# Fused attention and two MoE-style layers on one core: six chunks instead of seven in the first phase, two Strassen units of 768 tokens instead of one of 1024

## The chip, the core and the metric

The kernel runs on one core of a Trainium2 chip. Its time is the device time of that core in microseconds, and runs are compared by their median. TensorE (PE) does the matmuls; its weight loads are shown apart as PEld. VectorE (DVE), ScalarE (ACT) and GpSimd (POOL) do the elementwise work. SyncE (SP) issues nearly all DMAs, from one queue.

## The reference

All inputs are fp32. Attention without softmax has 8 batches, 8 heads, 576 positions and 64 features: `kv = k^T v` per head, `o = q kv`, then an RMS norm over the 64 features times `g_norm`. Its output, as 4608 tokens of 512 features, is `x`. Then:

```
a = x @ w1          # 512 x 1024
b = x @ w2          # 512 x 1024
x2 = ((a * b) @ w3) @ w_out          # 1024 x 1024, 1024 x 512
h = x2 @ moe2_w_in                   # 512 x 2048
out = (h * sigmoid(h)) @ moe2_w_out  # 2048 x 512
```

## The kernel before

Every fp32 matmul is made of three passes in the fp32r type, high x high, high x low and low x high, so each operand is split into a high and a low half (a cast on ScalarE, a subtraction on VectorE). The product `w3 @ w_out` is formed once at the start, so that the first layer is two matmuls: `a` and `b`, and `(a * b) @ wc`.

The 4608 tokens are 9 chunks of 512. **The first phase** computes the attention of all nine chunks. For the chunks in `PLAIN` it computes x2 at once by plain three-pass matmuls, in 8 steps a chunk. A step `j` has 12 matmuls into `pa`, 12 into `pb` and 12 into `x2ps` for the step before it (`g2_mm`), all 128x128 by 512 columns. ScalarE copies `pa` to `asb`, VectorE multiplies it with `pb`, and the product is split into `ch` and `cl`. The chunks in `LATER` only have their attention's output `x` stored to memory (`xd`).

Beside this the first phase converts weights for the second. A list of pieces (128x512 each) is worked off by `advance()`: load piece n+3, cast the high half of piece n-1 and scale piece n+1 on ScalarE, then on VectorE rebuild the bits of piece n (`cv_bits`), form Strassen sums where the piece is the second of its group (`block_sums`, role 1 of the roles 0, 1, 2), and subtract for the low half of piece n-1 (`cv_low`). The results are written to memory (`wbd`) by DMAs. The first 40 pieces belong to the resident weights. The 84 behind them are 28 groups of three: of kind "block" (two loads, the third piece has none) and, alternating with these for the first 24 groups, of kind "sum" (made from resident halves, no load). Between two steps' matmuls `ensure(done - 1)` calls `advance()` once: in each step behind `pa` ("piece A") and again behind the split of `ch` and `cl` ("piece B").

Attention is laid into this stream by hand. A gap is a third of a step; `event(gap, f, ...)` files a call under twice the gap, six such places a step, and `att_step(step, part)` calls what is filed. Part 0 comes behind `pa` (and takes what is filed for the last sixth of the step before too), part 1 behind piece A, part 2 behind the multiply of `pb` and `asb`, part 3 behind the split, part 4 behind `g2_mm`. Chunk c has these calls, in gaps from its base: `att_a`/`att_b` (q times kv, squares), `att_c` (sums of squares by matmul), `att_d` (ScalarE, the root), `att_e` (two VectorE operations and a split into `rh` and `rl`), `att_r` (spreads the root to PSUM banks `rb`), `att_x` (VectorE multiplies it on) and `att_f` (splits x, or stores it where c is in `LATER`). `kv_mm` makes the next batch's kv. All of these share two PSUM banks of the tag "att", which come round in the order of allocation.

**The second phase** takes x2, and for `LATER` first x, in units by one level of Strassen: seven products in place of eight. A unit has w columns for each half of its tokens, 2w tokens. Kind "A" runs the first layer for `LATER` (blocks a 0, b 0, a 1, b 1, out 0, out 1) and kind "B" the second layer (in 0 to 3, out 0 to 3). A block is 7 runs of 12 matmuls, 84 of w columns, and streams 7 weight tiles `w` of 512 KB. The last "out" block of a unit runs behind the first block of the next unit. On the engines every instruction is in the order in which the program issues it.

Of the kernel before, what the change touches and what calls it, by code (L numbers as in the profile page):

```python
# [16 lines left out]
B, H, S, D = 8, 8, 576, 64  # L17
# [6 lines left out]
NCH = NT // N  # L24
# [2 lines left out]
K2 = F2 // P  # L27
EPS = 1e-6

PLAIN = (0, 1, 2, 3, 5, 6, 7)  # L30
LATER = tuple(c for c in range(NCH) if c not in PLAIN)
UNITS = (("A", 512), ("B", 512), ("B", 512), ("B", 512), ("B", 384), ("B", 384))
HMAX = max(w for _, w in UNITS)
HOP = 512

# [38 lines left out]
def fused(ctx, tc, q, k, v, g, w1, w2, w3t, wo1, wb, out):  # L74
# [10 lines left out]
    def close(*names):  # L85
        for name in names:
            opened.pop(name).__exit__(None, None, None)
# [16 lines left out]
    def bank(tag, bufs, name):  # L104
        return ps.tile([P, N], F32, tag=tag, bufs=bufs, name=name)

    def split(h, l, x):
        nc.scalar.copy(out=h, in_=x)  # L108
        nc.vector.tensor_sub(out=l, in0=x, in1=h.bitcast(F32))
# [42 lines left out]
    done = 0  # L152
# [135 lines left out]
    def flush():  # L288
        due, writes[:] = list(writes), []
        for x in due:  # L290
            nc.sync.dma_start(**x)

    def advance():
        nonlocal done
        n = done
        flush()
        cv_load(n + 3)
        cv_high(n - 1)
        cv_scale(n + 1)
        cv_bits(n)  # L300
        block_sums(n)
        cv_low(n - 1)
        done += 1

    def ensure(n):

        while done < min(n + 2, len(pieces) + 1):
            advance()
# [134 lines left out]
    with tc.tile_pool(name="pro", bufs=2, side="right") as pro:  # L443
# [17 lines left out]
        for i in range(2 * K1):  # L461
            hf, j = divmod(i, K1)
# [24 lines left out]
        def w_out(m):  # L487
            split(wch[m], wcl[m], banks.pop(m))
# [66 lines left out]
    def g2_mm(c, j):  # L555
# [6 lines left out]
        if j == K1 - 1:  # L562
            for m in range(KD):
                if c != PLAIN[-1]:
                    o = at.tile([P, N], F32, tag="x2o", bufs=4, name=f"x2o{c}_{m}")
# [6 lines left out]
                else:  # L572
                    nc.scalar.copy(out=o, in_=x2ps[c][m])
                (nc.sync if c != PLAIN[-1] else nc.scalar).dma_start(out=x2d[c][:, m, :], in_=o)
            del x2ps[c]

    def g1_mm(ps_out, wh, wl, xh, xl):
        for kk in range(KD):
            s = slice(kk * P, (kk + 1) * P)
            passes(ps_out, wh[:, s], wl[:, s], xh[:, kk, :], xl[:, kk, :], kk == 0, kk == KD - 1)  # L580


    events = {}

    def event(gap, f, *args):
        events.setdefault(int(2 * gap), []).append(lambda: f(*args))

    gap = -6
    for c in range(1, NCH):
        if 1 < c < B:  # L590
            event(gap, kv_mm, c, [0, 1])
            event(gap, kv_load, c, [2, 3])
            event(gap + 3, kv_mm, c, [2, 3])
            event(gap + 3, kv_load, c, [4])
            event(gap + 6, kv_mm, c, [4])
            event(gap + 6, kv_out, c)
        if c + 1 < B:
            event(max(gap + 6, 2), kv_load, c + 1, [0, 1])
        if c > 1:
            for p in range(KD):  # L600
                event(gap_was + 11, q_load, c, p)
        for i in range(2):
            event(gap + 7 + 3 * i, att_a, c, i)
            event(gap + 7 + 3 * i, att_b, c, i)
        event(gap + 12, att_c, c)
        event(gap + 13, att_d, c)
        event(gap + 14, att_e, c)
        for i in range(2):
            event(gap + 17 + i, att_r, c, i)
            event(gap + 17 + i, att_x, c, i)  # L610
            event(gap + 17.5 + i + 1.5 * (c in LATER), att_f, c, i)
        gap_was = gap
        gap += 20 if c + 1 < B else 13

    def att_step(step, part):
        for n in range(6 * step + part - (part == 0), 6 * step + part + 1):
            for f in events.pop(n, ()):
                f()


    def b_pool(name, **more):
        return ctx.enter_context(tc.tile_pool(name=name, **{**dict(bufs=1, reuse_waits="tile"), **more}))


    blocks = []
    for u, (kind, _) in enumerate(UNITS):
        todo = ([("a", 0), ("b", 0), ("a", 1), ("b", 1), ("out", 0)] if kind == "A" else
                [("in", 0), ("in", 1), ("out", 0), ("in", 2), ("out", 1), ("in", 3), ("out", 2)])
        blocks.append((u, *todo[0]))
        if u > 0:  # L630
            blocks.append((u - 1, "out", NDB[UNITS[u - 1][0]] - 1))
        blocks += [(u, *x) for x in todo[1:]]
    blocks.append((len(UNITS) - 1, "out", NDB[UNITS[-1][0]] - 1))
    stream = [(b, n) for b in range(len(blocks)) for n in range(7)]
    wt = {}

    def w_load(at):
        if at >= len(stream):
            return
        b, n = stream[at]  # L640
        u, which, i = blocks[b]
        from_ = w_rest if at % WBUFS else w_first
        t = from_.tile([P, 2, 2, 2 * P], F32, tag="w", name=f"w{b}_{n}")
        nc.sync.dma_start(out=t, in_=wbd[i + WBD[(UNITS[u][0], which) if which == "out" else which]][:, RUNS[n][1]])
        wt[b, n] = t
# [4 lines left out]
    def half_pieces(u, h):  # L650

        kind, w = UNITS[u]
        t0 = 2 * sum(ww for k, ww in UNITS[:u] if k == kind) + h * w
# [8 lines left out]
    def x2_load(u):  # L662

        t = xr.tile([P, KD, 2, HMAX], F32, tag="x2r", name=f"x2r{u}")
        x2r[u] = t
        from_ = xd if UNITS[u][0] == "A" else x2d
        for h in range(2):
            for col, c, at0, n in half_pieces(u, h)[1]:
                for k0 in range(0, KD, 2):
                    r = slice(k0, k0 + 2)  # L670
                    yield nc.sync.dma_start(out=t[:, r, h, col:col + n], in_=from_[c][:, r, at0:at0 + n])
# [33 lines left out]
    def x2_ops(u):  # L705
        t, w = x2r.pop(u), UNITS[u][1]
        return Operands({f"b{i + 1}{h + 1}": t[:, 2 * i:2 * i + 2, h, :w] for i in range(2) for h in range(2)}, w,
                        lambda n: (x_first if n < 3 else x_rest).tile(
                            [P, 2, 2, HOP], F32R, tag=f"xo{n}", name=f"xo{u}_{n}"), f"x{u}",
                        [nc.gpsimd if u and n in (1, 3) else nc.vector for n in range(7)])  # L710

    prev = None
    for s_, c in enumerate(PLAIN):
        lastc = c == PLAIN[-1]
        xh, xl = xt.pop(c)
        for j in range(K1):
            step = s_ * K1 + j
            pa = bank("ab", 2, f"pa{c}_{j}")
            g1_mm(pa, w1h[j], w1l[j], xh, xl)
            att_step(step, 0)  # L720
            if s_ == 0 and j + 1 < K1:
                ensure(w12_piece[j + 1] - 1)
            elif not (lastc and j > 2):
                ensure(done - 1)
            att_step(step, 1)
            if s_ == 0 and j == 0:
                for m in range(half, K1):
                    w_out(m)
            asb = cp.tile([P, N], F32, tag="asb", bufs=1, name=f"asb{c}_{j}")
            nc.scalar.copy(out=asb, in_=pa)  # L730
            pb = bank("ab", 2, f"pb{c}_{j}")
            g1_mm(pb, w2h[j], w2l[j], xh, xl)
            ch = cp.tile([P, N], F32R, tag="ch", name=f"ch{c}_{j}")
            cl = cp.tile([P, N], F32R, tag="cl", name=f"cl{c}_{j}")
            nc.vector.tensor_mul(out=asb, in0=pb, in1=asb)  # L735
            att_step(step, 2)
            split(ch, cl, asb)
            ct[c, j] = ch, cl
            att_step(step, 3)
            if s_ == 0 and j + 1 < K1:  # L740
                ensure(w12_piece[j + 1])
            elif not (lastc and j > 2):
                ensure(done - 1)
            if lastc and j == 2:
                ensure(len(pieces))
            if lastc and j == 3:
                flush()
                nc.scalar.preload_act_table_set("silu_and_others")
                close("at", "cv", "stg")
                xr, w_first, tt, x_first = (b_pool(n) for n in ("xr", "w_first", "tt", "x_first"))  # L750
                list(x2_load(0))
                w_load(0)
            if lastc and j == 5:
                xops = {0: x2_ops(0)}
                xops[0].step(0)
                xops[0].sums()
            if lastc and j in (6, 7):
                xops[0].step(j - 5)
            if prev is not None:
                g2_mm(*prev)  # L760
            att_step(step, 4)
            prev = c, j
# [242 lines left out]
```

## Time and profile before

| | us |
|---|---|
| median of 3 runs | 1436.19 (1434.88 to 1437.12) |
| profiled execution | 1431.62 |
| its span, first to last instruction | 1429.5 |
| first phase, to the first matmul of the units | 609.7 |
| TensorE busy in the span | 1396.9 |
| VectorE busy | 916.2 |
| ScalarE busy | 665.1 |
| GpSimd busy | 311.6 |

The page gives for each engine the time in which an instruction of it ran. A matmul's row ends later than the next one starts, because they are pipelined, so its duration (390 ns) is not its cost; the distance from start to start is. The profiled execution is one run of its own, 4.6 us below the median of the others.

### The profile page before, as it was taken

The page shows a single profiled execution, that of the slowest core. Times are in us where ns is not written, and L with a number is a line of the kernel's source. Part 1 is how long each engine was busy: PE and PEld are TensorE (multiplying, and loading weights), DVE is VectorE, ACT ScalarE, POOL GpSimd, SP SyncE. Part 2 cuts the span into 40 slices and gives each one's busy share as a digit, 9 for nine tenths or more (in the row PEclk, how much of TensorE's full clock was granted, in tenths as well). Part 3 has the DMA queues.
Part 4 walks back from the last instruction along what each step waited for, and adds up shares of the span by engine and source line. Part 5 has one row for each costly group of instructions (what it writes and reads, how often), then busy time and mean ns, then how long its engine had stood idle before and what let it go on. Part 6 is the DMA issues. An engine that isn't in the chain of part 4 may idle for free.

```text
span 1429.5 us, 19284 instructions
## 1 busy us (share of the span) xinstructions
PE 1396.9 (98%) x7112; PEld 1150.0 (80%) x7112; DVE 916.2 (64%) x1263; ACT 665.1 (47%) x1064; POOL 311.6 (22%) x143
## 2 busy tenths in 40 slices
PE   7789999999999999999999999999999999999998
PEld 4567777777777777888878787887878789999998
DVE  7767475565656674343775668566865676678568
ACT  7766445443444562232535354443535354543443
POOL 0000000000000001104533526224532442345222
PEclk9999999999999999999999999999999999999999
DMA  9655566768595767076677666866686668878876
GB/s 334 226 174 171 193 205 229 255 211 278 195 296 179 254 197 269 18 244 199 193 232 266 191 191 203 295 193 185 193 287 194 189 205 288 288 244 253 287 246 205
DMA packets 149725, 320.05 MB, mean 224 GB/s; under 512 B 14208, under 2 KB 72576, under 8 KB 149632
## 3 DMA queue, kind: packets, MB, share of 16 engines
q1 hardware_dynamic: 149056, 317.78, 68.5%
q8 instruction: 57, 0.93, 0.3%
q10 hardware_dynamic: 576, 1.05, 0.2%
q14 instruction: 36, 0.29, 0.1%
HBM read 246.42 MB, written 72.35 MB: 223 GB/s over the span
## 4 chain that ended last, share of the span: by engine, by line
PE 93%; DVE 2%; DMA 2%; issue 1%; ACT 1%; SPq 0%; DVEq 0%; ACTq 0%
PE ps L795 56%; PE pb L113 4%; PE x2ps L113 4%; PE pa L113 4%; PE pb L115 4%; PE pb L114 3%; PE x2ps L115 3%; PE pa L115 3%; PE x2ps L114 3%; PE pa L114 3%; DMA raw<-w3t_l 1%; PE kvps L338 1%; PE o L370 1%; PE rb L419 1%; DVE z L201 1%
## 5 line engine op out<-in xcount | busy, mean ns | idle before, releaser
L795 PE MATMUL ps<-xo,w 128*128 128x512 f32 (+1 forms) x2016 | 425.4, 371 | 0.1
L795 PEld LDWEIGHTS ps<-xo,w 128*128 128x128 f32 x2016 | 368.8, 188 | 53.7 <-ACT u L827 1.3
L795 PE MATMUL ps<-go,w 128*128 128x512 f32 (+1 forms) x1848 | 392.4, 370 | 5.1 <-issue 5.1
L795 PEld LDWEIGHTS ps<-go,w 128*128 128x128 f32 x1848 | 335.8, 188 | 58.3 <-issue 12.2
L699 DVE TENSOR_TENSOR go<-g,go 128x1024 fp32r<-128x1024 f32 (+1 forms) x110 | 156.2, 1424 | 112.9 <-ACT go L698 112.5
L805 DVE TENSOR_TENSOR c<-ps,c 128x512 f32<-128x512 f32 (+1 forms) x260 | 154.3, 632 | 24.6 <-PE ps L795 24.4
L686 POOL TENSOR_TENSOR x_t<-x2r 128x1024 f32<-128x1024 f32 (+1 forms) x12 | 30.3, 2522 | 564.4 <-DMA w<-wbd 563.9
L686 POOL TENSOR_TENSOR g_t<-g 128x1024 f32<-128x1024 f32 (+1 forms) x44 | 113.0, 2569 | 108.6 <-ACT g L838 62.5
L698 ACT CAST go<-g 128x1024 fp32r<-128x1024 f32 (+1 forms) x110 | 105.0, 974 | 46.2 <-PE ps L795 35.0
L686 POOL TENSOR_TENSOR g<-g,g_t 128x1024 f32<-128x1024 f32 (+1 forms) x22 | 48.4, 2200 | 342.8 <-DVE go L699 342.8
L735 DVE TENSOR_TENSOR asb<-pb,asb 128x512 f32<-128x512 f32 x56 | 38.7, 690 | 124.5 <-PE pb L115 118.3
L699 DVE TENSOR_TENSOR go<-g_t,go 128x1024 fp32r<-128x1024 f32 (+1 forms) x44 | 93.6, 2127 | 20.7 <-ACT go L698 20.7
L827 ACT COPY s<-ps 128x512 f32<-128x512 f32 (+1 forms) x40 | 21.8, 545 | 154.3 <-PE ps L795 154.3
L108 ACT CAST ch<-asb 128x512 fp32r<-128x512 f32 x56 | 35.0, 626 | 123.1 <-DVE asb L735 123.1
L113 PE MATMUL pb<-xh,w2h 128*128 128x512 f32 x224 | 89.5, 400 | 0.3 <-ACT w2h L217 0.3
L113 PE MATMUL pa<-xh,w1h 128*128 128x512 f32 x224 | 89.5, 400 | 0.0
L113 PE MATMUL x2ps<-ch,wch 128*128 128x512 f32 x224 | 89.4, 399 | 0.0
L115 PE MATMUL pb<-xh,w2l 128*128 128x512 f32 x224 | 87.4, 390 | 1.4 <-DVE w2l L230 1.4
L115 PE MATMUL pa<-xh,w1l 128*128 128x512 f32 x224 | 87.3, 390 | 0.0
L115 PE MATMUL x2ps<-ch,wcl 128*128 128x512 f32 x224 | 87.3, 390 | 0.0
L114 PE MATMUL pb<-xl,w2h 128*128 128x512 f32 x224 | 87.3, 390 | 0.0
L114 PE MATMUL x2ps<-cl,wch 128*128 128x512 f32 x224 | 87.3, 390 | 0.0
(113 smaller groups left out, 1892.9 us busy)
## 6 DMA issues: line engine op xcount, KB each, us to landing
w<-wbd SPq DMA_DIRECT2D x322, 512.0 KB, 4.2
wbd<-bh SPq DMA_DIRECT2D x72, 256.0 KB, 3.4
raw<-wb_l SPq DMA_DIRECT2D x32, 512.0 KB, 5.3
wbd<-s SPq DMA_DIRECT2D x56, 256.0 KB, 3.1
q<-q_l SPq DMA_DIRECT2D x36, 256.0 KB, 4.5
raw<-w3t_l SPq DMA_DIRECT2D x16, 512.0 KB, 5.8
k<-k_l SPq DMA_DIRECT2D x32, 256.0 KB, 4.3
v<-v_l SPq DMA_DIRECT2D x32, 256.0 KB, 4.7
```

Of the source, the lines that this page charges most:

```text
L108: nc.scalar.copy(out=h, in_=x)
L113: nc.tensor.matmul(out=ps_out, lhsT=ah, rhs=bh, start=first, stop=False)
L114: nc.tensor.matmul(out=ps_out, lhsT=ah, rhs=bl, start=False, stop=False)
L115: nc.tensor.matmul(out=ps_out, lhsT=al, rhs=bh, start=False, stop=last)
L201: nc.vector.scalar_tensor_tensor(out=z, in0=hi, scalar=0x80000000, in1=z, op0=ALU.bitwise_and, op1=ALU.bitwise_or)
L686: nc.gpsimd.tensor_tensor(out=x, in0=x if a == place else self.src[a], in1=x if b == place else self.src[b], op=ALU.subtract)
L698: nc.scalar.copy(out=t[:, 0, :, :self.w], in_=x)
L699: self.cuts[n].tensor_tensor(out=t[:, 1, :, :self.w], in0=x, in1=t[:, 0, :, :self.w].bitcast(F32), op=ALU.subtract)
L735: nc.vector.tensor_mul(out=asb, in0=pb, in1=asb)
L795: mm = lambda a, bb, start, stop: nc.tensor.matmul(out=o, lhsT=a, rhs=bb, start=start, stop=stop, skip_group_check=True)
L805: eng.tensor_tensor(out=out_, in0=a, in1=b, op=ALU.add)
L827: nc.scalar.copy(out=t[nm, d], in_=o)
```

## The change

Chunk 3 and chunk 7 go to `LATER`, chunk 4 comes back to `PLAIN`: six plain chunks, 48 steps instead of 56, and `LATER` = (3, 7, 8). The one unit A of 2 x 512 tokens becomes two of 2 x 384. An even step calls `advance()` twice for piece B; an odd one once as before. The attention of a chunk has 18 gaps instead of 20 (11 instead of 13 for the last), with `att_r`, `att_x` and `att_f` one gap nearer to `att_e`. The later place of `att_f` for chunks in `LATER` no longer holds for the last chunk. An assertion at build time says that nothing of attention is left at the step where its buffers are closed.

```
-PLAIN = (0, 1, 2, 3, 5, 6, 7)
+PLAIN = (0, 1, 2, 4, 5, 6)
 LATER = tuple(c for c in range(NCH) if c not in PLAIN)
-UNITS = (("A", 512), ("B", 512), ("B", 512), ("B", 512), ("B", 384), ("B", 384))
+UNITS = (("A", 384), ("A", 384), ("B", 512), ("B", 512), ("B", 512), ("B", 384), ("B", 384))
...
         for i in range(2):
-            event(gap + 17 + i, att_r, c, i)
-            event(gap + 17 + i, att_x, c, i)
-            event(gap + 17.5 + i + 1.5 * (c in LATER), att_f, c, i)
+            event(gap + 16 + i, att_r, c, i)
+            event(gap + 16 + i, att_x, c, i)
+            event(gap + 16.5 + i + 1.5 * (c in LATER and c + 1 < NCH), att_f, c, i)
         gap_was = gap
-        gap += 20 if c + 1 < B else 13
+        gap += 18 if c + 1 < B else 11
...
             elif not (lastc and j > 2):
-                ensure(done - 1)
+                for _ in range(2 - j % 2):
+                    ensure(done - 1)
             if lastc and j == 2:
                 ensure(len(pieces))
             if lastc and j == 3:
+                assert not events
                 flush()
```

## Rows read from the trace of the kernel before

**Rows 1.** The page: the span, the engines' busy time, and the chain of work that ended last, by engine.
```profile
span 1429.5 us, 19284 instructions
...
PE 1396.9 (98%) x7112; PEld 1150.0 (80%) x7112; DVE 916.2 (64%) x1263; ACT 665.1 (47%) x1064; POOL 311.6 (22%) x143
...
PE 93%; DVE 2%; DMA 2%; issue 1%; ACT 1%; SPq 0%; DVEq 0%; ACTq 0%
```

**Rows 2.** The timeline of TensorE in the second phase, matmuls in a row merged: start us, length us, what, shapes, count. The first row is the blocks a 0, b 0, a 1 and b 1 of unit 0; then its out 0, its out 1 and what follows it; then in 2, out 1 and in 3 of the first unit of 384 columns.
```profile
609.71 76.32 PE L795 MATMUL ps<-xo,w 128*128 128x512 f32 x336
685.87 19.20 PE L795 MATMUL ps<-go,w 128*128 128x512 f32 x84
...
723.95 11.04 PE L795 MATMUL ps<-go,w 128*128 128x512 f32 x48
...
744.09 19.20 PE L795 MATMUL ps<-xo,w 128*128 128x512 f32 x84
...
1232.39 14.72 PE L795 MATMUL ps<-xo,w 128*128 128x384 f32 x84
1246.95 8.48 PE L795 MATMUL ps<-go,w 128*128 128x384 f32 x48
...
1262.46 14.72 PE L795 MATMUL ps<-xo,w 128*128 128x384 f32 x84
```

**Rows 3.** The timeline of TensorE: the first matmul into `pa` in two steps that follow each other in the last plain chunk, where no attention is left.
```profile
558.03 0.39 PE L113 MATMUL pa<-xh,w1h 128*128 128x512 f32 x1
...
566.19 0.39 PE L113 MATMUL pa<-xh,w1h 128*128 128x512 f32 x1
```

**Rows 4.** Busy time by stage: stretch, length, busy us and count of PE, PEld, DVE, ACT and POOL, granted TensorE clock, DMA share, GB/s. The stretch in which the last 81 pieces are converted, and a step in which loads for the second phase arrive.
```profile
158.70:549.90 391.20, 389.61 (x2182) 297.49 (x2181) 246.86 (x464) 187.44 (x345) 0.00 (x0) 1.00 0.70 229
...
558.00:566.20 8.20, 8.20 (x38) 6.76 (x37) 1.38 (x2) 1.21 (x2) 0.00 (x0) 1.00 1.02 363
```

**Rows 5.** The timeline of TensorE around the end of chunk 5's attention: a step's first `pa`, the second pair of `rb`, the next step's first `pa` and first `pb`, and `kv_mm` of the next batch.
```profile
369.50 0.39 PE L113 MATMUL pa<-xh,w1h 128*128 128x512 f32 x1
...
378.66 0.50 PE L419 MATMUL rb<-rh,spread 32*128 32x512 f32 x2
...
379.32 0.50 PE L113 MATMUL pa<-xh,w1h 128*128 128x512 f32 x1
...
382.18 0.39 PE L113 MATMUL pb<-xh,w2h 128*128 128x512 f32 x1
...
384.99 1.15 PE L338 MATMUL kvps<-v,k 128*64 128x64 f32 x32
```

**Rows 6.** The timeline of VectorE over the same stretch, from the step before: `att_e` (L405 to `rl`), `cl`, a "sum" piece of role 1 (L181 to L280), the multiply (L735), `att_x` 0 (L426), `cl`, `att_f` 0 (`xl`), a "block" piece of role 0 (L201 to L280), `att_x` 1.
```profile
367.05 0.69 DVE L735 TENSOR_TENSOR asb<-pb,asb 128x512 f32<-128x512 f32 x1 [2.43 <-PE pb L115]
367.65 0.68 DVE L405 SCALAR_TENSOR_TENSOR u<-s,u 128x512 f32<-128x512 f32 x1
...
369.75 0.69 DVE L109 TENSOR_TENSOR rl<-u,rh 128x512 fp32r<-128x512 f32 x1 [0.69 <-ACT rh L108]
370.36 0.68 DVE L109 TENSOR_TENSOR cl<-asb,ch 128x512 fp32r<-128x512 f32 x1
370.96 0.69 DVE L181 TENSOR_TENSOR t<-w2h,w2l 128x512 f32<-128x512 f32 x1
...
373.03 0.69 DVE L280 TENSOR_TENSOR s<-s,bh 128x512 fp32r<-128x512 f32 x1
375.21 0.69 DVE L735 TENSOR_TENSOR asb<-pb,asb 128x512 f32<-128x512 f32 x1 [1.49 <-PE pb L115]
375.81 1.28 DVE L426 TENSOR_TENSOR ob<-rb,ob 128x512 f32<-128x512 f32 x2
377.01 0.68 DVE L109 TENSOR_TENSOR cl<-asb,ch 128x512 fp32r<-128x512 f32 x1
377.61 1.29 DVE L109 TENSOR_TENSOR xl<-ob,xh 128x512 fp32r<-128x512 f32 x2
378.81 0.68 DVE L201 SCALAR_TENSOR_TENSOR z<-raw,z 128x512 uint32<-128x512 uint32 x1
...
380.74 1.28 DVE L426 TENSOR_TENSOR ob<-rb,ob 128x512 f32<-128x512 f32 x2
```

**Rows 7.** The timeline of VectorE at chunk 6: a "block" piece of role 1 from its first operation, and what follows it.
```profile
440.37 0.68 DVE L201 SCALAR_TENSOR_TENSOR z<-raw,z 128x512 uint32<-128x512 uint32 x1
...
444.10 1.28 DVE L109 TENSOR_TENSOR xl<-ob,xh 128x512 fp32r<-128x512 f32 x2
```

**Rows 8.** The instructions that read or write `x2ps`: the x2 evictions on VectorE, with duration in ns (min/median/max), first and last start.
```profile
L571 DVE COPY x2o<-x2ps x14: 681/684/692, 170.5 to 609.9; 128x512 f32<-128x512 f32 x14
```

**Rows 9.** Waits: TensorE's in the first phase from 100 us on (us in total, times, longest); who waited for `att_x` (us, times); VectorE's multiply for `pb` while pieces are converted.
```profile
PE kvps L338 <- DMA v<-v_l: 1.6, 2, 1.0
...
  PEld rb L419: 1.4, 4
...
DVE asb L735 <- PE pb L115: 68.8, 30, 4.7
```

**Rows 10.** DMA issues: what, queue, count, KB each, median us from issue to landing. The weight tiles of the second phase, and the raw pieces of the first.
```profile
w<-wbd SPq DMA_DIRECT2D x322, 512.0 KB, 4.2
...
raw<-wb_l SPq DMA_DIRECT2D x30, 512.0 KB, 5.3
```

## Prediction, made before the changed kernel was run

> **What bounds the kernel now.** I read the page first, then the pace of the matmuls, then who waits for whom around the attention. On the page TensorE is busy for 98% of the span and the chain that ended last is 93% TensorE [rows 1]. Matmul busy time flatters, so the reader should look at starts. In the second phase 336 matmuls of 512 columns take 685.87 - 609.71 = 76.16 us, four blocks of 19.04 us, 226.7 ns each; 84 of 384 columns take 1246.95 - 1232.39 = 14.56 us, 173.3 ns each [rows 2]. A plain step without attention takes 566.19 - 558.03 = 8.16 us for its 36 matmuls, the same 226.7 ns [rows 3]. So both phases run at TensorE's issue pace at a granted clock of 1.00. In the stretch in which weight pieces are converted (158.7 to 549.9 us) TensorE is busy for 389.6 of 391.2 us, VectorE for 246.9 us, 63% [rows 4]. That is an average; what matters is whether VectorE is late at the moments at which TensorE needs something of it.
>
> **The matmuls.** One plain chunk less is 288 matmuls, 288 x 226.7 = 65.28 us off. A unit of kind A has 6 blocks of 84. One of 1024 tokens costs 6 x 19.04 = 114.24 us, two of 768 cost 12 x 14.56 = 174.72 us: 60.48 us on. The block "out 1" has a hiccup: 744.09 - 723.95 = 20.14 us at 512, 1.10 over the pace, and 1262.46 - 1246.95 = 15.51 us at 384, 0.95 over [rows 2]. Two of the second for one of the first: +0.80. Together -65.28 + 60.48 + 0.80 = -4.0 us. A bound on the far side is no hiccup in either new unit (-5.9), on the near side a hiccup in all four "out" blocks (-2.1).
>
> [...]
>
> **What rides along.** The weight stream of the second phase grows by 42 loads of 512 KB. The units of 384 columns at the end of the kernel already stream at that rate without a wait of TensorE in "in" blocks [rows 2], so I take nothing; if one load were late, at most its 4.2 us to landing [rows 10]. Attention's work, the pieces and the stores are the same in number; only their spacing changes. The loads of unit 0 now wait behind chunk 8's stores in step 43 instead of running ahead; the first cast of them comes two steps (16 us) later, so nothing.
>
> **The waits in the first phase.** VectorE works strictly in program order. In one step the order is: piece A, the multiply `asb`, whatever `att_step` 2 brings, `cl`, `att_step` 3, the B pieces, `att_step` 4. With 18 gaps a chunk is exactly six steps, so every chunk from 1 to 7 has the same phase: `att_e` in part 4 of an even step (which now has two B pieces ahead of it), `att_r`/`att_x` 0 in part 2 and 1 in part 4 of the odd step behind it, then `pa`, and at once `kv_mm` of the next chunk in part 0. `kv_mm` needs a bank of the tag "att", and the one that comes round is that of `rb` 2, free after the first multiply of `att_x` 1. Before there was a gap more (2.72 us of matmuls) in front of it.
>
> How close is it? In chunk 5 of before the phase of r and x is by chance the same. The second `rb` pair starts at 378.66, `pa` ends at about 382.1, `pb` goes in between, and `kvps` starts at 384.99 [rows 5]. The first multiply of x 1 ends at 380.74 + 0.69 = 381.43 [rows 6]: 3.6 us to spare. Without `pb` in between it would have 0.7 us to spare, and that with a light piece in B: from 378.81 to 380.74, 1.93 us. A piece of role 1 costs more, since `block_sums` is in it: 440.37 to 444.10, 3.73 us, in a "block" group [rows 7], and 370.96 to 373.72, 2.7 us, in a "sum" group [rows 6]. By the count of pieces (43 are done after step 7, the last 3 of them of the 84 behind the first 40; then 5 every two steps), the B of the odd step is always of role 1: "block" for chunks 2, 4, 6 and 7, "sum" for 3 and 5.
>
> Chunk 4, with 0 at the start of the odd step: in rows 5 and 6 the step starts at 369.50 and the multiply at 375.21, 5.71 later, so the even step's multiply is at 5.71 - 8.16 = -2.45 and its `cl` done 2.0 later at -0.45. B ("sum", role 1, then an empty role 2) 2.7: 2.25. `att_e`, from 367.65 to 370.36 in [rows 6], 2.7: 4.95, just ahead of `pb`'s end at 5.44. Piece A (role 0, 1.93): 6.9. Multiply, x 0 (1.2), `cl`, the two subtractions of `att_f` 0 (1.2): 10.5. B (3.73): 14.2. First multiply of x 1: 14.9. TensorE is at `kv_mm` at 382.1 - 369.5 = 12.6. It waits 2.3 us.
>
> The others by the same walk. Chunks 2 and 6: the two x2 evictions (2 x 0.65, [rows 8]) of the chunk that ends stand ahead of `att_e`, so `rl` is late by 0.4, `rb` 2 by 0.5, and `kv_mm` by 2.6: 3.5 each. Chunk 5: roles 1 and 2 of a "block" group ahead of `att_e` (4.3) make `rl` late by 0.8 and `kv_mm` by 1.5: 2.3. Chunk 3 goes to memory and has no `att_f` subtractions: 1.0. Chunk 7: 0.8 + 0.5, and `att_a` of chunk 8, which needs both banks, 2.0: 3.3. Chunk 1 (pieces of 2 us, two a step): 0.5. Sum 7.0 + 2.3 + 2.3 + 1.0 + 3.3 + 0.5 = 16.4 us. That TensorE does wait on these banks is seen in before: `rb` waited four times for `att_x`, 1.4 us [rows 9].
>
> Bounds: nothing (every chunk like chunk 5 of before, 0.7 to spare) below; above, VectorE's own wait inside a piece for ScalarE or a late load added to each of seven chunks, 2 us a chunk, 30 us. I take 16.4, since each part of the walk is a duration of a row.
>
> [...] The rows agree: x 0, `cl`, `xl`, the piece and x 1 stand in program order [rows 6].
>
> **The sum.** -4.0 + 16.4 = +12.4 us on the profiled execution's 1431.62 us (2.1 over its span of 1429.5): 1444.0. The median of the runs shown, 1436.19, lies 4.6 above the profiled one; on it 1448.6 us.
>
> **Rivals.**
> *VectorE keeps up.* The place is the first multiply of x 1; it decides whether it ends within 3.4 us (382.1 - 378.7) of `rb` 2's start [rows 5]. For it: VectorE is idle 37% of the stretch, and in before 30 waits of its multiply for `pb` (68.8 us in all) show that it is mostly early [rows 9]. Against it: that slack is not at this place. Then -4.0 us, 1432.2: faster.
> *Half of it.* If the walk overstates each piece's lag by 2 us (work that I placed late runs while VectorE waits for `pb`), each chunk's wait shrinks by so much, to some 5 us in all (1.5 + 1.5 + 0.3 + 0.3 + 1.3), and it nearly cancels: 1437.
> *Transfers on top.* The pieces and attention move in 33 steps what took 41: 229 GB/s become about 229 x 41/33 = 285, where the densest stretch of before moved 363 at a share of 1.02 [rows 4]. `kv_mm` already waited once for `v`, 1.6 us [rows 9], and a raw piece takes 5.3 us to land [rows 10] while the distance from issue to use shrinks to half a step in even steps. If each of the six next chunks has such a wait of 1.6 us or a late piece, another 10 us: 1459.
>
> **Chances.** The forecast 0.55; transfers on top 0.2; half of it 0.13; VectorE keeps up 0.12. About 0.2% (2.9 us) is what a measurement of this kernel can tell from no change. The forecast's own range is 9 to 20 us of waits: 1441 to 1452. The range that leaves out the case "keeps up" and the far end of the transfers, 1434 to 1462. Faster by over 0.2%: 0.12; within 0.2%: 0.13; slower: 0.75.
>
> **What would show it.** In the profile after: `ps` blocks of 14.56 us for units 0 and 1 and the first of them starting some 65 us earlier plus the first phase's waits; TensorE's wait at `kvps` on VectorE's `ob`, six times, 1 to 4 us each, and at `rb` on `rl`; VectorE about 75% busy while pieces run. Wrong if `kvps` and `rb` show no waits on VectorE, or if VectorE's role 1 piece is done ahead of `rb` 2; or if blocks of unit 0 or 1 wait for `w`.

## The result and the profile after

The changed kernel takes 1450.7 us (median of 4 runs, 1449.3 to 1457.7), the kernel before beside it 1435.8: ratio 1.0113, 95% interval 1.0092 to 1.0134. It is slower, by about 15 us; 1448.6 was forecast. The profiled execution is the one of 1457.65 us, 7 us above the median.

The page of after; the rows answer to [rows 1]:

```profile
span 1455.7 us, 20075 instructions
...
PE 1409.1 (97%) x7328; PEld 1186.4 (81%) x7328; DVE 936.7 (64%) x1320; ACT 675.7 (46%) x1099; POOL 332.6 (23%) x157
...
PE 85%; DVE 8%; DMA 3%; issue 2%; ACT 2%; SPq 0%; DVEq 0%; ACTq 0%
```

VectorE's busy share is 64% as before, yet its part in the chain that ended last went from 2% to 8%: hardly more work, but work in a worse place.

The span grew by 26.25 us, which split into three stretches (differences are taken before rounding). The reader needs three marks: the first matmul of step 2 (102.0 us before, 111.5 after), the first matmul of unit 0 (609.71 and 572.08), and the end of the span.

- Up to step 2: +9.5 us.
- From step 2 to unit 0: 507.7 us became 460.6, so -47.1 where the matmuls alone give -65.3. TensorE loses 18.2 us more in the first phase than it did, in waits and behind them.
- From unit 0 to the end: 819.8 us became 883.6, so +63.9 where +61.3 was predicted.

The first is no part of the change. Busy time by stage of the opening (columns as in [rows 4]), after first, then before:

```profile
40.00:111.50 71.50, 62.24 (x315) 43.13 (x314) 43.15 (x68) 44.00 (x79) 0.00 (x0) 0.83 0.54 173
```
```profile
40.00:102.00 62.00, 51.32 (x310) 35.52 (x309) 42.04 (x67) 42.91 (x77) 0.00 (x0) 1.00 0.60 196
```

TensorE's granted clock was 0.83 there, 1.00 in before. In the thirteen profiled executions of this study step 2 starts anywhere from 101.7 to 111.5 us, also with the old chunks and units (110.1 in e2, 108.1 in e11). So profiles are compared below from step 2 on: 1327.4 us before, 1344.2 after, +16.8.

TensorE's waits on other engines in the first phase of after, 80 to 640 us (us in total, times, longest); they answer to [rows 9]:

```profile
PE kvps L338 <- DVE ob L426: 8.8, 4, 2.5
...
PE o L370 <- DVE ob L426: 1.2, 1, 1.2
PE rb L419 <- ACT rh L108: 1.2, 3, 0.4
PE kvps L338 <- DMA v<-v_l: 1.1, 1, 1.1
PE rb L419 <- DVE rl L109: 0.8, 5, 0.2
```

The first line is the wait that the prediction named. It now stands at `kv_mm`, in the place where before had a gap of matmuls. This is chunk 4 on VectorE, then on TensorE (timelines, columns as in [rows 5, 6]):

```profile
308.37 1.28 DVE L426 TENSOR_TENSOR ob<-rb,ob 128x512 f32<-128x512 f32 x2
...
310.16 1.29 DVE L109 TENSOR_TENSOR xl<-ob,xh 128x512 fp32r<-128x512 f32 x2
311.36 0.68 DVE L201 SCALAR_TENSOR_TENSOR z<-raw,z 128x512 uint32<-128x512 uint32 x1
...
314.49 0.68 DVE L280 TENSOR_TENSOR s<-s,bh 128x512 fp32r<-128x512 f32 x1
315.09 1.28 DVE L426 TENSOR_TENSOR ob<-rb,ob 128x512 f32<-128x512 f32 x2
```
```profile
309.64 0.55 PE L419 MATMUL rb<-rh,spread 32*128 32x512 f32 x2
...
312.98 0.39 PE L115 MATMUL pa<-xh,w1l 128*128 128x512 f32 x1
315.83 1.97 PE L338 MATMUL kvps<-v,k 128*64 128x64 f32 x32 [2.46 <-DVE ob L426]
317.73 0.80 PE L113 MATMUL pb<-xh,w2h 128*128 128x512 f32 x1
```

`rb` 2 starts at 309.64 and takes 0.55 us. VectorE takes `cl`, `att_f` 0's two subtractions and the whole role-1 piece (311.36 to 315.17) first, and its multiply of `att_x` 1 comes at 315.09. `kvps` starts at 315.83, when the first of the two multiplies is done (315.09 and 0.68 us, their median in after: 315.77). In between TensorE has no `pb` to do, only `pa`, and stands for 2.46 us.

### The profile page after: what moved, and what is told of

It is laid out like the page before. It is cut to its first block, busy times and chain, and to the rows that moved or that the text cites. A ratio compares the mean times of both kernels' runs of the same rounds, so it can differ in the third digit from the quotient of the medians.

```text
span 1455.7 us, 20075 instructions
## 1 busy us (share of the span) xinstructions
PE 1409.1 (97%) x7328; PEld 1186.4 (81%) x7328; DVE 936.7 (64%) x1320; ACT 675.7 (46%) x1099; POOL 332.6 (23%) x157
## 4 chain that ended last, share of the span: by engine, by line
PE 85%; DVE 8%; DMA 3%; issue 2%; ACT 2%; SPq 0%; DVEq 0%; ACTq 0%
PE ps L797 58%; PE pb L113 3%; PE pb L115 3%; PE pb L114 3%; PE x2ps L113 2%; PE x2ps L114 2%; PE x2ps L115 2%; PE pa L113 2%; PE pa L114 2%; PE pa L115 2%; PE kvps L338 1%; PE o L370 1%; DVE z L201 1%; DMA w<-wbd 1%; DMA raw<-w3t_l 1%
## 5 line engine op out<-in xcount | busy, mean ns | idle before, releaser
L797 PE MATMUL ps<-xo,w 128*128 128x384 f32 (+1 forms) x2352 | 466.7, 358 | 0.7 <-DMA w<-wbd 0.5
L797 PEld LDWEIGHTS ps<-xo,w 128*128 128x128 f32 x2352 | 422.2, 188 | 41.8 <-ACT u L829 1.3
L797 PE MATMUL ps<-go,w 128*128 128x384 f32 (+1 forms) x2016 | 412.9, 363 | 7.1 <-issue 7.1
L699 DVE TENSOR_TENSOR go<-g,go 128x768 fp32r<-128x768 f32 (+1 forms) x120 | 163.3, 1365 | 120.9 <-ACT go L698 120.5
L686 POOL TENSOR_TENSOR x_t<-x2r 128x768 f32<-128x768 f32 (+1 forms) x14 | 32.8, 2342 | 543.7 <-DMA w<-wbd 543.2
L686 POOL TENSOR_TENSOR g_t<-g 128x768 f32<-128x768 f32 (+1 forms) x48 | 119.3, 2486 | 131.4 <-DVE g L879 65.6
L698 ACT CAST go<-g 128x768 fp32r<-128x768 f32 (+1 forms) x120 | 110.9, 945 | 48.3 <-PE ps L797 40.1
L686 POOL TENSOR_TENSOR g<-g,g_t 128x768 f32<-128x768 f32 (+1 forms) x24 | 50.9, 2122 | 354.4 <-DVE go L699 354.4
L699 DVE TENSOR_TENSOR go<-g_t,go 128x768 fp32r<-128x768 f32 (+1 forms) x48 | 96.5, 2011 | 21.0 <-ACT go L698 21.0
L735 DVE TENSOR_TENSOR asb<-pb,asb 128x512 f32<-128x512 f32 x48 | 33.1, 690 | 104.6 <-PE pb L115 101.7
L114 PE MATMUL pa<-xl,w1h 128*128 128x512 f32 x192 | 74.8, 390 | 0.0
```

What stands on the lines that cost most here:

```text
L114: nc.tensor.matmul(out=ps_out, lhsT=ah, rhs=bl, start=False, stop=False)
L686: nc.gpsimd.tensor_tensor(out=x, in0=x if a == place else self.src[a], in1=x if b == place else self.src[b], op=ALU.subtract)
L698: nc.scalar.copy(out=t[:, 0, :, :self.w], in_=x)
L699: self.cuts[n].tensor_tensor(out=t[:, 1, :, :self.w], in0=x, in1=t[:, 0, :, :self.w].bitcast(F32), op=ALU.subtract)
L797: mm = lambda a, bb, start, stop: nc.tensor.matmul(out=o, lhsT=a, rhs=bb, start=start, stop=stop, skip_group_check=True)
```

## The experiments

Every run's time is beside the kernel before on the same chip. "From step 2" is the profiled execution's time from the first matmul of step 2 to the end, less that of before (1327.4 us); it leaves the uneven opening out, but is one execution of each kernel. "From unit 0" is its part from the first matmul of unit 0 on, less before's 819.8 us; with the added unit, 60.5 us of it are matmuls at pace.

| kernel | median us | before us | ratio, 95% | from step 2 | from unit 0 |
|---|---|---|---|---|---|
| after | 1450.7 | 1435.8 | 1.0113 (1.0092 to 1.0134) | +16.8 | +63.9 |
| e1: k/v work a gap later | 1449.5 | 1434.9 | 1.0098 (1.0067 to 1.0129) | +21.1 | +64.6 |
| e2: 18 gaps alone | 1436.1 | 1434.9 | 1.0007 (0.9994 to 1.0019) | -0.2 | |
| e3: 2.5 pieces alone | 1445.5 | 1434.9 | 1.0070 (1.0043 to 1.0097) | +7.9 | |
| e4: both, old units | 1455.7 | 1434.9 | 1.0143 (1.0119 to 1.0167) | +20.3 | |
| e5: after, pieces last | 1445.9 | 1434.9 | 1.0073 (1.0052 to 1.0093) | +10.4 | |
| e6: e4, pieces last | 1447.8 | 1434.9 | 1.0082 (1.0056 to 1.0108) | +13.6 | |
| e7: e5, quiet steps | 1436.5 | 1434.6 | 1.0009 (0.9994 to 1.0024) | +0.3 | +64.4 |
| e8: e7, k/v on another queue | 1436.0 | 1434.6 | 1.0008 (0.9993 to 1.0023) | +0.5 | |
| e9: e7, second phase eased | 1432.9 | 1435.7 | 0.9987 (0.9971 to 1.0003) | -4.0 | +60.1 |
| e10: e9, sums on VectorE | 1429.2 | 1435.2 | 0.9949 (0.9931 to 0.9968) | -9.2 | +54.8 |
| e11: before, sums on VectorE | 1429.7 | 1435.2 | 0.9965 (0.9951 to 0.9980) | -6.2 | -5.9 |

### Which part does it: e2, e3, e4

e2 is the kernel before with the new gaps, e3 with the new number of pieces, e4 with both; chunks and units stay.

```
 e2, e4:  -        event(gap + 17 + i, att_r, c, i)
          +        event(gap + 16 + i, att_r, c, i)
          ...
          -        gap += 20 if c + 1 < B else 13
          +        gap += 18 if c + 1 < B else 11
 e3, e4:  -                ensure(done - 1)
          +                for _ in range(2 - j % 2):
          +                    ensure(done - 1)
```

> The kernel before with the 18 gaps alone: seven plain chunks, the old units, one piece at a time in each step. Theory: with two pieces a step the period of six steps holds 12 pieces, so the piece between the two att_x calls is always of the same role, 0 (1.93 us), and x 1 is done about 0.7 us ahead of kv_mm: within 2 us of the kernel before, 1434 to 1438. If the shorter distance alone did it, whatever the piece: 1444 to 1452.

> The kernel before with the 2.5 pieces a step alone: 20 gaps, seven plain chunks, the old units. VectorE's work and the transfers of the pieces are as dense as in the changed kernel, but kv_mm stands two gaps behind x 1. Theory: 0 to 3 us over the kernel before, 1435 to 1439. Rival, dense transfers: 8 to 12 us over it, 1444 to 1448, with waits of TensorE on k and v or of ScalarE on raw pieces.

> The kernel before with both, 18 gaps and 2.5 pieces, on the old chunks and units. Theory: all the waits of the changed kernel's first phase and none of its exchange of matmuls, so 4 us more than the changed kernel: 1450 to 1457. Rival, the short units carry the loss: as the kernel before, 1435 to 1439.

The gaps alone cost nothing: with one piece a half step VectorE is on time even at six steps a chunk. Both together, with the old chunks and units, cost the most, and show the same line of waits as after: `kvps` on `ob`, 8.2 us in five. So the price sits in pieces and gaps together. The other half of the change (one chunk less, two smaller units) takes 5.0 us off e4 by the medians, 3.6 from step 2 on, with other waits in the two.

e3 missed what my theory expected and came out where its rival had put it, at 1444 to 1448 us with waits for late data. It cost about 10 us, through another door. Waits of TensorE in e3 (100 to 610 us), then SP's queue and the wait itself:

```profile
PE kvps L338 <- DMA v<-v_l: 6.0, 2, 5.8
```
```profile
329.30 2.39 SPq L574 DMA_DIRECT2D x2d<-x2o  x4
331.75 1.17 SPq L431 DMA_DIRECT2D xd<-ob  x2
333.01 0.54 SPq L323 DMA_DIRECT2D k<-k_l  x1
333.59 0.58 SPq L323 DMA_DIRECT2D v<-v_l  x1
```
```profile
340.13 1.12 PE L338 MATMUL kvps<-v,k 128*64 128x64 f32 x16 [5.78 <-DMA v<-v_l]
```

The loads of k and v stand in SP's queue behind stores of what VectorE makes, and in these rows SP issues them in the program's order, the stores from 329.30 and `v` at 333.59: late stores, late loads. Between 322 and 336 us the queue waited 4.1 us for one `t` of VectorE's; the issues of k and v take 0.5 to 0.6 us each. The load of that `v` was issued at 333.59, less than 1 us before TensorE came to `kvps` (334.35), and landed 6.5 us after its issue; the median of such loads in e3 is 5.0. So most of the 5.8 us is the late issue, and some 1.5 us the slower landing, at a DMA share of 1.08 in those 6.5 us. Behind the wait TensorE's granted clock was 0.51 (337 to 344 us), which is part of the price too.

### Moving the wait: e1

e1 leaves the pieces and puts `kv_mm` behind a `pb` again.

```
 -            event(gap, kv_mm, c, [0, 1])
 -            event(gap, kv_load, c, [2, 3])
 -            event(gap + 3, kv_mm, c, [2, 3])
 -            event(gap + 3, kv_load, c, [4])
 +            event(gap + 1, kv_mm, c, [0, 1])
 +            event(gap + 1, kv_load, c, [2, 3])
 +            event(gap + 4, kv_mm, c, [2, 3])
 +            event(gap + 4, kv_load, c, [4])
```

> The changed kernel with one thing moved: the first two calls of kv_mm of each batch (and the loads behind them) are filed one gap later, so that the 12 matmuls into pb stand between pa and kv_mm again, as in the kernel before. Chunks, units, pieces and the 18 gaps stay. Theory (VectorE reaches the first multiply of att_x 1 up to 2.5 us after TensorE wants the bank for kv_mm): the six waits at kvps (8.8 us in all, and the slow matmuls behind the longest of them, some 3 us) go, 1437 to 1440 us, 10 to 13 below the changed kernel. What is left are the short waits at rb and the one at chunk 8's att_a. Rival, dense transfers: waits come from late k, v and pieces, so kv_mm waits as before the move, 1448 to 1451. Rival, the short units: the loss is in the second phase, 1448 to 1451.

Nothing was gained: the time is that of the rivals. TensorE's waits in e1, 100 to 610 us, the first line:

```profile
PE kvps L338 <- DMA v<-v_l: 9.1, 3, 4.9
```

The waits on `ob` at `kvps` are gone, as meant; in their place TensorE waits for `v`. My edit had a part in it: it left two gaps, where there were three, between the load of the last tile and its use. The other part is the queue again, where the load of `v` comes at the end of a row of stores:

```profile
440.35 0.33 SPq L191 DMA_DIRECT2D wbd<-wch  x1
...
445.13 0.48 SPq L323 DMA_DIRECT2D k<-k_l  x1
445.66 0.59 SPq L323 DMA_DIRECT2D v<-v_l  x1
```

Here it is not VectorE that the stores wait for: SP's queue waited 1.9 us for a raw piece to land at 440.35, and then issued without a stop; ScalarE waited 6.93 us for the same piece. And the waits were not the whole price. The steps with these three waits took 5.5, 3.4 and 7.9 us longer than in e9, and only 9.1 of these 16.8 us are wait; the granted clock was 0.57 from 203 to 211 us and from 449 to 457, 0.66 from 326 to 331. So e1 says that this one wait can be moved, not that VectorE's lateness has no other customers.

### Order of the work on VectorE: e5, e6, e7

e5 (on after) and e6 (on e4) issue the B pieces behind `att_step` 4 instead of ahead of it, so that `att_x` 1 comes before them.

```
 -            elif not (lastc and j > 2):
 -                for _ in range(2 - j % 2):
 -                    ensure(done - 1)
              ...
              att_step(step, 4)
 +            if not (s_ == 0 and j + 1 < K1) and not (lastc and j > 2):
 +                for _ in range(2 - j % 2):
 +                    ensure(done - 1)
              ...
```

> The changed kernel with the B pieces of each step issued last, behind att_step 4 in place of ahead of g2_mm. Same pieces, same gaps, same distance from the second att_x to kv_mm; only the order on VectorE and ScalarE differs: att_e and the second att_x stand ahead of the pieces. Theory (the order in VectorE's queue is the cause): by the walk the first multiply of x 1 ends at 11.2 to 12.5 us in a step in which TensorE comes to kv_mm at 12.6, and rl is there 2 us ahead of rb. The waits at kvps, rb and chunk 8's o on VectorE fall from 12 us to under 2, the half-speed matmuls behind them go: 1433 to 1437 us, no different from the kernel before, since the exchange of matmuls was worth only about 1 us by the blocks of the changed kernel's profile. Rival, VectorE has too much work in these steps whatever the order: the waits move to the next multiply or to the pieces, 1445 to 1451. Rival, late k and v: new waits at kvps on v as in the run with kv_mm a gap later, 1440 to 1447.

> The run with 18 gaps and 2.5 pieces on the old chunks and units, with the B pieces issued last in the step as in the run beside it. Theory: the 20 us that this pair cost go, 1434 to 1438 us, the kernel before again; the difference to the run beside it is then the exchange of matmuls with its hiccups alone, 0 to 2 us. Rivals as there: 1445 to 1455.

Both gained (5 and 8 us), a third of what I expected or a little more. e5's waits of TensorE, 100 to 610 us:

```profile
PE rb L419 <- DVE ob L426: 4.9, 5, 1.4
PE kvps L338 <- DMA v<-v_l: 4.2, 3, 2.4
```

The pieces that were ahead of `att_x` 1 are now ahead of the next step's work: the second `rb` waits for `att_x` 0. The order alone moves the lateness by half a step. e7 therefore also takes work out of the two steps of attention's tail: 2 pieces in `att_e`'s step, 1 in `att_r`'s and 3 in each of the other four, 15 in six steps as in after.

```
 -            elif not (lastc and j > 2):
 +            elif not (lastc and j > 2) and step % 6 != 3:
                  ensure(done - 1)
              ...
              att_step(step, 4)
 +            if not (s_ == 0 and j + 1 < K1) and not (lastc and j > 2):
 +                for _ in range(1 if step % 6 in (2, 3) else 2):
 +                    ensure(done - 1)
              ...
```

> The run with the pieces last, with the same 84 pieces spread otherwise over the six steps of a chunk's attention: two in the step of att_e, one in the step of att_r, three in each of the other four. Theory (TensorE waits only where VectorE has pieces to do between att_e and the second att_x): the waits at rb on ob (4.9 us in the run before it) go, only late v is left (4.2 us there, here 2 to 6 us, since pieces stand closer around the loads of k and v): 1438 to 1443 us. Rival, the sum of VectorE's work in the first phase is too much for 48 steps, wherever it stands: waits of 8 us or more at other places, 1445 to 1450.

All of e7's waits of TensorE between 100 and 610 us:

```profile
PE pb L113 <- DVE asb L735: 1.5, 1, 1.5
PE pb L115 <- DVE w2l L230: 1.4, 1, 1.4
PE rb L419 <- ACT rh L108: 0.3, 1, 0.3
PE rb L419 <- DVE rl L109: 0.2, 1, 0.2
```

With the same pieces, chunks, units and gaps the waits are gone: 443.5 us from step 2 to unit 0, against 507.7 - 65.3 = 442.4 with no more waits than before had. The waits for `v`, which I expected to stay at 2 to 6 us, went with the others, and e7 came out below its expected range. DMA moved at least as much as in the runs that had such waits: 271 GB/s between 158.7 and 480 us, e3 269, e5 265, e1 264. So the mean rate did not make `v` late. That VectorE's lateness did, passed on by SP's queue, is shown for e3 alone; e7 also moved the pieces' own loads and stores in that queue. e8 is e7 with the loads of k and v of batches 2 to 7 on GpSimd's queue.

```
 -                nc.sync.dma_start(out=t[:n], in_=src[b, j * P:j * P + n, :])
 +                (nc.sync if b < 2 else nc.gpsimd).dma_start(out=t[:n], in_=src[b, j * P:j * P + n, :])
```

> The run beside it, with the loads of k and v for batches 2 to 7 issued from GpSimd's queue, which is empty in the first phase, and no longer behind the pieces' loads and stores in SyncE's. Theory (late v is SyncE's queue: 9 to 40 issues of 0.45 us and their waits on ScalarE and VectorE stand ahead): the waits at kvps on v go to under 1 us, 1434 to 1438 us, the time of the kernel before, since the exchange of matmuls with its hiccups is worth 1 us. Rival, the transfers themselves are slow because the DMA engines are full: v is as late as in the run beside it, no gain.

It gains nothing more. But e7 had no wait for `v` left to lose, so e8 cannot tell a late queue from slow transfers. The run that could, this edit on e1, e3 or e5, was not made.

But e7, with those waits gone, is no faster than before. The exchange of matmuls was to bring 4 us; with 64.4 us more from unit 0 on, against 65.3 less ahead of it, it brings 0.9.

### The second phase: e9, e10, e11

In after and e7 "out 1" of unit 1, a block of 14.56 us at pace, takes 17.7 us. TensorE in after, from that block's first matmul to the next block:

```profile
752.79 8.51 PE L797 MATMUL ps<-go,w 128*128 128x384 f32 x48
763.17 2.32 PE L797 MATMUL ps<-go,w 128*128 128x384 f32 x12 [1.86 <-issue]
766.22 4.42 PE L797 MATMUL ps<-go,w 128*128 128x384 f32 x24 [0.73 <-issue]
770.48 19.24 PE L797 MATMUL ps<-xo,w 128*128 128x512 f32 x84
```

The profile puts the idle time before two of the pieces down to "issue". After's VectorE, then GpSimd in the same block (start us, length us):

```profile
754.34 0.96 DVE L699 TENSOR_TENSOR go<-g,go 128x768 fp32r<-128x768 f32 x1 [1.85 <-ACT go L698]
756.97 2.56 DVE L699 TENSOR_TENSOR go<-g_t,go 128x768 fp32r<-128x768 f32 x1 [0.74 <-ACT go L698]
760.38 2.21 DVE L699 TENSOR_TENSOR go<-g,go 128x768 fp32r<-128x768 f32 x1
763.45 2.20 DVE L699 TENSOR_TENSOR go<-g,go 128x768 fp32r<-128x768 f32 x1
```
```profile
756.29 2.41 POOL L686 TENSOR_TENSOR g_t<-g 128x1024 f32<-128x1024 f32 x1 [4.62 <-ACT g L840]
758.78 2.99 POOL L686 TENSOR_TENSOR g<-g 128x1024 f32<-128x1024 f32 x1
761.86 2.98 POOL L686 TENSOR_TENSOR g_t<-g 128x1024 f32<-128x1024 f32 x1
```

TensorE goes on at 763.17 and 766.22, 0.58 and 0.57 us behind the ends of the last two subtractions (762.59 and 765.65), as it would if `go` is what it waits for. The same subtraction takes 0.96 us alone and 2.20 to 2.56 us when GpSimd's sums of the next unit run. Add 0.96 us to the end of the GpSimd sum that was under way: 758.70 + 0.96 = 759.66, 761.77 + 0.96 = 762.73, 764.84 + 0.96 = 765.80. The three subtractions end at 759.53, 762.59 and 765.65, each 0.13 to 0.15 us sooner. They look as if they stood until the sum was done. That they did is my reading of these three ends, which agree with it to 0.15 us; no run shows what held them.

e9 is e7 with two edits: the first sums of a 512 unit's g behind a 384 unit go to VectorE, where they come ahead of `out 1`'s subtractions, and in units of kind A the weight and x2 loads go out in every second run.

```
              ...
 +                    if nxt[0] > 0 and UNITS[nxt[0] - 1][1] < w and nxt[2] == 0:
 +                        gops[nxt[0], nxt[2]].adds = nc.vector
                      gops[nxt[0], nxt[2]].sums()
 +                    gops[nxt[0], nxt[2]].adds = nc.gpsimd
              ...
 -            if load:
 +            if load and (kind == "B" or n % 2 == 0):
                  next(loads, None)
```

> The run with the quiet tail, with two things moved in the second phase. The three Strassen sums for the first g of the unit of 512 columns that follows a unit of 384 go from GpSimd to VectorE, into their place in the block behind; and the x2 loads beside a unit of kind A are issued in every second run and not in six runs one after another. Theory (out 1 of the second unit A is 3.1 us over its pace because GpSimd runs those sums in it and VectorE's subtraction of 128x768 takes 2.2 us beside them, 0.96 without; the blocks b 0 to b 1 are 1.2 over because w tiles land behind the bunched x2 loads): out 1 takes 14.6 to 16 us in place of 17.7, b 0, a 1 and b 1 together 43.7 to 44.0 in place of 44.9, in 1 of the next unit stays within 0.5 us of 19.08; 3 us in all, 1432 to 1435 us, 1 to 3 below the kernel before. Rival, the hiccup belongs to a narrow block behind a wide one, whoever does the sums: out 1 stays at 17 to 18 us, 1435 to 1437.

The block in e9:

```profile
730.10 14.75 PE L798 MATMUL ps<-go,w 128*128 128x384 f32 x84
744.69 19.24 PE L798 MATMUL ps<-xo,w 128*128 128x512 f32 x84
```

It starts at 730.10 and the next at 744.69, 14.59 us. From unit 0 on e9 takes 60.1 us more than before, e7 64.4. The 2.7 us by which e9's median is below before are not clear of the noise (the interval reaches 1.0003).

The hiccups of 1.10 and 0.95 us in before [rows 2] look to be of the same kind. In the one of 1.10 two subtractions of 128x1024, 1.23 us alone, take 2.24 and 2.21 and end at 734.51 and 737.84, 0.15 us sooner than the GpSimd sum's end plus 1.23; TensorE goes on 0.70 and 0.71 us behind them. e10 moves three of the four sums of each g (`t3`, `t1`, `t2`) to VectorE in every unit; `t4` stays on GpSimd. e11 does that alone on the kernel before.

```
 -                    if nxt[0] > 0 and UNITS[nxt[0] - 1][1] < w and nxt[2] == 0:
 -                        gops[nxt[0], nxt[2]].adds = nc.vector
 +                    gops[nxt[0], nxt[2]].adds = nc.vector
```

> The kernel of e9_second_phase with every sum of the Strassen operands of g (the calls of g_ops that went to GpSimd) on VectorE; nothing is left out. Theory (GpSimd's sums slow VectorE's go subtractions that run beside them, and TensorE waits for those at the head of blocks): the hiccups of about 1.1 us at the heads of the 512-wide out blocks and 0.95 us at the 384-wide ones, eleven in all, go, the subtractions stand near 1.2 us at 1024 wide and 0.96 us at 768 wide throughout, and the time is 1420 to 1428 us. Rival (VectorE has no room for the sums: 66 more of about 1.25 us each, before the subtractions that TensorE waits for): new waits of TensorE on go, 1432 to 1440 us.

> The kernel before with the same move alone (all g_ops sums from GpSimd to VectorE), nothing left out. Theory of the slowed subtractions: its hiccups of 1.1 us at the heads of the out blocks go too, 7 to 9 us in all, 1426 to 1430 us; then this gain is independent of the change of chunks and units. Rival (VectorE has no room): 1436 to 1444 us.

(The expectation says every sum; it is three of four, 72 in e10 and 66 in e11.) Both are faster than the kernel before, by 6.0 and 5.5 us, and e10 is 1.2 above its expected range; the intervals of the two overlap. Block "out 1" of unit 0 in e11, which was 744.09 - 723.95 = 20.14 us in [rows 2], and one of e11's sums by duration in ns (min/median/max):

```profile
729.71 19.20 PE L796 MATMUL ps<-go,w 128*128 128x512 f32 x84
```
```profile
L687 DVE TENSOR_TENSOR g_t<-g x44: 946/1218/1227, 670.7 to 1401.7; 128x1024 f32<-128x1024 f32 x28, 128x768 f32<-128x768 f32 x16
```

Before had these on GpSimd:

```profile
L686 POOL TENSOR_TENSOR g_t<-g x44: 1844/2415/3382, 646.8 to 1403.4; 128x1024 f32<-128x1024 f32 x28, 128x768 f32<-128x768 f32 x16
```

A sum of 1.84 to 3.38 us is one of 0.95 to 1.23 on VectorE, which had the room at nearly every place. The move takes GpSimd from VectorE's side and halves the sums at once, so these two runs do not tell which of both is worth how much. Over the second phase the blocks' excess over pace falls from 12.1 us in before to 6.2 in e11, and from 11.6 in e9 to 6.4 in e10.

Not all of it goes. e10's out 1 at 805.26 keeps a hiccup of 1.3 us, where GpSimd still makes sums of the next unit's x beside VectorE's subtractions (GpSimd, VectorE, TensorE):

```profile
813.17 2.41 POOL L687 TENSOR_TENSOR x_t<-x2r 128x1024 f32<-128x1024 f32 x1 [1.23 <-DVE go L700]
814.15 2.52 DVE L700 TENSOR_TENSOR go<-g,go 128x1024 fp32r<-128x1024 f32 x1
817.37 8.42 PE L798 MATMUL ps<-go,w 128*128 128x512 f32 x36 [1.06 <-issue]
```

The sum ends at 815.58; with the 1.21 us of such a subtraction alone that makes 816.79. This one ends at 816.67, and TensorE goes on 0.70 us behind it. No run moves these sums. And out 2 of the last unit grew from 0.9 to 1.6 us over pace in both runs: there, from 1399.67 to 1402.61 in e11, VectorE's own three sums stand ahead of the subtraction.

So the gain of some 6 us is independent of the change. On top of it, the change in its mended form (e7's order, e9's loads) adds 3.0 us by one profile of each from step 2 (-9.2 against -6.2); the medians do not tell e10 and e11 apart.

## Why the prediction was right, point by point

**The matmuls.** The pace held: 572.08 to 630.35 us for four blocks, 58.27 where 4 x 14.56 = 58.24:

```profile
572.08 58.43 PE L797 MATMUL ps<-xo,w 128*128 128x384 f32 x336
```

**The hiccup.** This term was mis-sized. I gave each new "out 1" the 0.95 us of the units at the end. Unit 0's had none: GpSimd's sums for unit 1 were done at 654.06, ahead of the block (659.46), and the subtractions beside it took 0.95 to 0.96 us. Unit 1's had 3.13: GpSimd's sums for the 1024 tokens behind it take 2.41 to 2.99 us, where those beside the hiccup of 0.95 took 1.85 to 2.46. Its b 0, a 1 and b 1 took 44.77 us, 1.09 over pace, with two waits for `w` in them (0.33 and 0.21 us), which I had put at nothing; a block of unit 0 or 1 that waits for `w` was one of my signs of being wrong, and this one came. So the exchange is worth -65.3 + 63.9 = -1.4 us in after, not -4.0.

**The waits in the first phase.** Predicted 16.4, measured 18.2. The wait at `kvps` on `ob` came four times, not six, with 1.4 to 2.5 us. VectorE was busy for 67% of 158.7 to 505 us, not about 75%: the place was right, the load overstated. By chunk, as the excess of its two steps over the same steps where nothing waits (9.82 and 9.60 us in most chunks of e9, 9.56 for the second of chunk 7):

| chunk | predicted | measured |
|---|---|---|
| 1 | 0.5 | 0 |
| 2 | 3.5 | 0.8 + 4.1 |
| 3 | 1.0 | 1.0 |
| 4 | 2.3 | 0 + 3.9 |
| 5 | 2.3 | 0.9 + 1.5 |
| 6 | 3.5 | 1.0 + 2.6 |
| 7 | 3.3 | 1.3 + 1.9 |

The first number is the step of `rl` and `rb`, the second that of `kv_mm` or, for chunk 7, of `att_a`. Where only the wait counts, the walk was within 0.3 us: 2.46 for 2.3 in chunk 4, 1.43 for 1.5 in chunk 5. What was missing in chunks 2 and 4 is the clock behind the wait (below), 1.7 + 1.4 = 3.1 us. One late `v` cost a step 1.2 us more, which I had left to a rival. With it the steps add up to 20.2 us; before had some 2 us of its own, such as the 1.6 for `v` in [rows 9] (two waits, not the one that I read there).

**The sum.** -4.0 + 16.4 = +12.4 was forecast. From step 2 on the profile has -1.4 + 18.2 = +16.8, and the medians differ by 14.9. The terms came out 2.6 and 1.8 us too low. That the second is so near is in part luck: the walk left out 3.1 us of clock and 1.2 of late `v`, and did not take off the 2 us of waits that before already had.

**VectorE in program order.** e5 and e7 are the test: with the same instructions in another order, 5 and 14 us come back. The pieces' work on ScalarE and their DMAs move with them, so the order on VectorE is not the only thing that changes. That the role-1 piece ahead of `att_x` 1 is the cause is shown by the rows above and by e5 (the waits of `kvps` on `ob` go), that it is not the whole of it by what e5 keeps.

**The rivals.** "VectorE keeps up" fell with the first line of waits; it holds for the gaps without the pieces (e2). "Half of it" fell too. "Transfers on top" was half right: loads are late in e1, e3 and e5. It is not the mean rate, as e7 shows without any at as high a one. In e3 VectorE's late stores hold them up in SP's queue; in e1's longest wait the queue stood behind a raw piece that landed late, and what began that lateness stays open.

## What to carry to other kernels

When work is packed into fewer steps, the average share of the busy engine can say nothing, as here: 64% before and after. Walk the one queue in program order at the point where the next engine needs its result, and count what stands ahead. A lateness moves: one wait undone (e1, e5) came out at the next customer, and in e3 through SP's queue of DMAs as "late data"; only less work in the tight steps (e7) made it go. And look at what GpSimd does beside VectorE before giving it work "for free": here subtractions of 0.96 us became 2.20 to 2.56.

## What the runs showed of the hardware that I had not expected

**VectorE beside GpSimd.** In after's out 1 of unit 1 a VectorE subtraction of 128x768 took 0.96 us alone and 2.20 to 2.56 us beside a GpSimd sum, and ended 0.13 to 0.15 us sooner than that sum's end plus its own 0.96 us.

**The clock behind a wait.** After two of the three waits of 2.46 us at `kvps` TensorE came back at a lower granted clock. Around chunk 2's it was 0.76, and the matmuls behind the wait start 1.28 us apart in threes, 427 ns each, 1.88 times the 226.7 ns at a granted clock of 1.00.

```profile
194.89 1.15 PE L338 MATMUL kvps<-v,k 128*64 128x64 f32 x32 [2.46 <-DVE ob L426]
...
196.92 0.63 PE L115 MATMUL pb<-xh,w2l 128*128 128x512 f32 x1
...
198.20 0.63 PE L115 MATMUL pb<-xh,w2l 128*128 128x512 f32 x1
```
```profile
192.40:199.60 7.20, 4.75 (x42) 3.88 (x42) 4.92 (x10) 2.22 (x4) 0.00 (x0) 0.76 0.32 114
```

Chunk 4's was the same (0.76 from 312 to 319 us); behind chunk 6's, as long, the clock stayed at 1.00 (435.5 to 443). What tells them apart stays open. The step with chunk 2's `kv_mm` took 13.72 us where e9's takes 9.60: 2.46 of wait and 1.7 of clock.
